# A linear-attention and expert-attention kernel: another source for its filler matmuls, and another cut of its first batch

## The chip, the cores and the metric

The kernel runs on one core of one Trainium2 chip. Its engines run side by side, each through its own list of instructions in order: TensorE (PE in the profile; PEld are its weight loads), VectorE (DVE), ScalarE (ACT), GpSimd (POOL) and SyncE (SP), which here issues all transfers (DMA). The metric is device microseconds of one execution; less is better.

## The reference

Two stages. First a linear attention with a complex decay for each channel, for 4 batches, 8 heads, 768 steps and 48 channels a head:

```python
mag = np.sqrt(a_re * a_re + a_im * a_im)
scale = np.minimum(mag, 0.999) / (mag + 1e-06)
a_re_n, a_im_n = (a_re * scale, a_im * scale)
for t in range(S):
    new_re = ar * S_re - ai * S_im          # ar, ai: step t of a_re_n, a_im_n
    new_im = ar * S_im + ai * S_re
    S_re, S_im = (new_re + k_t v_t^T, new_im)
    y[:, :, t] = q_t S_re
```

Its output, 768 steps by 384 columns for each batch, is the x of the second stage: four experts, each a causal softmax attention (`wq`, `wk`, `wv`, `wo`, 64 columns), added up for each step with the weights of the two experts that a gate (`w_gate`) ranks highest.

## The kernel before

**The first stage, in chunks.** The decay is written as magnitude and angle: their running sums over a chunk turn q and k into decayed, rotated q and k, and what is left are matmuls over chunks of 128 steps. The 384 columns lie as three groups j of 128 partitions. Elementwise work on `ab` (the decays) and `qk` goes through the helpers `quotients`, `arcs`, `magnitudes`, `angles`, `sines`, `products`, on VectorE, ScalarE and GpSimd. `regroup` (transfers `fm<-qk`) puts the columns of two heads together (four pairs g; pair 0 lies in group j=0 alone, pair 1 in j=0 and 1, pair 2 in j=1 and 2, pair 3 in j=2). For each pair and each k (256 steps, two chunks) `head` transposes k (`pk`, to `kts`) and makes the chunk's scores (`psc`, masked to `pts` with `keep`), `state` makes the carried state (`pu`, `sum`, `tst`), and `tail` the output (`yu`, to `x`; pair 3 goes by `yt` and transfers `x<-yt`).

**The second stage**, `moe(b)`: `proj` makes q and k of two experts at a time (`pp`, to `qka`), 512 and then 256 steps wide, nine matmuls each; `vproj` (`pv`) the values and the gate's logits; `maxpass` the row maxima (`pm`, `mx`), `mrow` (`pmr`) turns them; then `score` (`psS`, to `pe`), `av` (`po`), `total` (`dn`), `norm`, `wo` (`pw`).

**The order.** No helper issues an instruction at once. `Work` collects them as a numbered list, and `run` issues them in the order of the written list `ORDER`, a permutation of all of them. Each engine's instructions follow each other in that order, and SyncE's transfers too. `ROOMS` says which of its buffers each tile gets. `WARM` says ahead of which numbers how many filler matmuls (`warm`) are put: 128 by 128 weights, 512 columns, into a PSUM bank that nobody reads. There are 244 of them; 172 stand ahead of number 171, the first matmul of the first `head`. What they read is set by

```python
    nc.warm = keep, mask[:, :512]
```

where `keep` and `mask` are made from `iota` by VectorE: `keep` (number 2) is at place 178 of `ORDER`, among the elementwise work, `mask` at 7 and 104.

In the first batch the elementwise work is cut: `quotients` and `arcs` for all three groups, for k=0 and then for k=1 and 2 together, then the other helpers and the heads k by k. The batches 1 to 3 go group by group, all 768 steps at once. Loads are SyncE's first instructions: `ab` and `qk` of the first batch in two parts (k=0; k=1 and 2), the weights `wst`, and `vt`.

Of the kernel before, what the change touches and what calls it, by code (L numbers as in the profile page):

```python
# [390 lines left out]
def attention_moe(ctx: ExitStack, tc: tile.TileContext, ak, vk, w, out):  # L391
# [489 lines left out]
    for g in range(NP):  # L881
        load_v(0, g)
    load_w()
    for c in PARTS:
        for f in (quotients, arcs):
            for j in range(3):
                f(0, j, *c)
# [76 lines left out]
```

## Time and profile before

| | us |
|---|---|
| median of the runs shown (3) | 502.98 |
| lowest and highest of them | 499.4, 504.44 |
| the profiled execution | 498.99 |
| its span, first to last instruction | 497.3 |

| engine | busy us | share of the span | instructions |
|---|---|---|---|
| TensorE, matmuls | 437.3 | 88% | 3720 |
| VectorE | 338.4 | 68% | 788 |
| ScalarE | 332.2 | 67% | 762 |
| GpSimd | 239.2 | 48% | 225 |

Between the profiled execution's time and its span lie 1.7 us. The profile's page has the sum for each engine, the span in 40 slices, and the chain of work that ended last; the views of the trace (timeline, waits, windows, groups by form) show single instructions. Times in them count from the span's start.

### The profile page before, as it was taken

How to read it: one execution, taken by the hardware profiler on the slowest of the kernel's cores; microseconds unless marked ns; L12 is line 12 of the kernel's file. 1: busy time of each engine (PE TensorE's matmuls, PEld its weight loads, DVE VectorE, ACT ScalarE, POOL GpSimd, SP SyncE). 2: the span in 40 equal slices, each digit the busy share in tenths (PEclk: the TensorE clock that was granted, in tenths of full speed). 3: DMA queues.
4: the chain of work that ended last, by engine and by line, in shares of the span. 5: the costliest groups of instructions: out<-in, count | busy, mean ns of one | idle time of the engine just before them, and what ended most of it. 6: DMA issues, size and time to landing. Idle time of an engine off the chain costs nothing.

```text
span 497.3 us, 10026 instructions
## 1 busy us (share of the span) xinstructions
PE 437.3 (88%) x3720; PEld 334.0 (67%) x3720; DVE 338.4 (68%) x788; ACT 332.2 (67%) x762; POOL 239.2 (48%) x225
## 2 busy tenths in 40 slices
PE   0009999899898899999898999999999999999995
PEld 0004446777658667787797877878988887887565
DVE  4793007858876999985388989778887752566711
ACT  5992006859966888886685899867868556234453
POOL 3643004425842457769732379847434416302780
PEclk9999999999999989999899999999999999999999
DMA  8901003575187827218345492366405302001002
GB/s 286 347 1 42 1 0 85 154 205 141 21 227 172 194 87 171 87 28 212 65 120 152 96 242 96 92 158 180 109 12 125 97 7 59 18 32 65 18 1 95
DMA packets 22943, 53.46 MB, mean 107 GB/s; under 512 B 3344, under 2 KB 9584, under 8 KB 22768
## 3 DMA queue, kind: packets, MB, share of 16 engines
q1 hardware_dynamic: 22896, 52.83, 38.9%
q8 instruction: 29, 0.48, 0.4%
q14 instruction: 18, 0.15, 0.1%
HBM read 26.74 MB, written 4.72 MB: 63 GB/s over the span
## 4 chain that ended last, share of the span: by engine, by line
PE 60%; ACT 11%; DVE 11%; DMA 7%; POOL 4%; issue 3%; SPq 2%; POOLq 0%; DVEq 0%; ACTq 0%
PE psS L387 9%; PE warm L380 9%; PE pp L387 7%; PE po L387 7%; PE yu L387 6%; PE psc L387 6%; ACT qk L387 5%; PE pw L387 4%; PE pu L387 3%; DVE qk L387 3%; PE pv L387 3%; ACT ab L387 3%; PE pm L387 2%; DMA ab<-in_ak_dram 2%; SPq L387 2%
## 5 line engine op out<-in xcount | busy, mean ns | idle before, releaser
L380 PE MATMUL warm<-mask,keep 128*128 128x512 bf16 x244 | 58.3, 392 | 37.6 <-DVE carry L387 37.5
L387 POOL TENSOR_TENSOR pe<-pe 128x512 f32<-128x512 f32 (+1 forms) x64 | 80.5, 1259 | 20.6 <-PE po L387 17.7
L380 PEld LDWEIGHTS <-keep 128*128 128x128 bf16 x244 | 24.0, 101 | 66.3 <-DVE keep L387 37.5
L387 DVE TENSOR_TENSOR pts<-psc,keep 128x512 f32<-128x512 f32 x48 | 32.7, 682 | 44.7 <-PE psc L387 42.2
L387 ACT ACTIVATE ab<-ab 128x768 f32<-128x768 f32 (+2 forms) x90 | 56.5, 644 | 8.4 <-DVE ab L387 4.7
L387 ACT ACTIVATE qk<-qk 128x768 f32<-128x768 f32 (+3 forms) x126 | 59.7, 500 | 2.6 <-DVE qk L387 2.1
L387 POOL TENSOR_TENSOR qk<-qk,ab 128x256 f32<-128x256 f32 (+1 forms) x24 | 29.4, 1226 | 60.8 <-ACT ab L387 52.1
L387 ACT ACTIVATE pe<-psS 128x512 f32<-128x512 f32 (+2 forms) x96 | 47.3, 542 | 16.9 <-PE psS L387 14.1
L387 PE MATMUL psc<-fm 96*128 96x128 f32 x384 | 54.2, 286 | 2.0 <-ACT kts L387 1.0
L387 POOL TENSOR_TENSOR qk<-qk 128x768 f32<-128x768 f32 (+1 forms) x27 | 36.4, 1354 | 38.2 <-ACT qk L387 37.6
L387 POOL TENSOR_SCALAR_AFFINE_SELECT pe<-pe 128x256 f32<-128x256 f32 x48 | 26.3, 561 | 57.6 <-ACT pe L387 55.9
L387 DVE CUSTOM_DVE_ANT_0 pm<-pm,mask 128x384 f32<-128x384 f32 (+4 forms) x96 | 46.9, 512 | 10.0 <-PE pm L387 9.8
L387 PEld LDWEIGHTS psc<-fm 96*128 96x128 f32 x384 | 47.3, 194 | 7.8 <-ACT kts L387 2.3
L387 ACT ACTIVATE kts<-pk 128x384 f32<-128x384 f32 (+1 forms) x48 | 20.3, 431 | 44.9 <-PE pk L387 44.7
L387 PE MATMUL pp<-x,whi 128*128 128x512 f32 (+1 forms) x192 | 45.2, 353 | 5.4 <-DMA x<-yt 4.0
L387 ACT ACTIVATE tst<-sum,fm 96x48 f32<-96x48 f32 x128 | 38.9, 326 | 16.3 <-DVE sum L387 16.2
L387 PE MATMUL psS<-qka 64*128 64x256 f32 (+3 forms) x480 | 46.9, 303 | 0.1
L387 PE MATMUL po<-pe,v 128*64 128x256 f32 (+3 forms) x320 | 45.4, 397 | 0.0
L387 PEld LDWEIGHTS psS<-qka 64*128 64x128 f32 x480 | 37.2, 185 | 7.0 <-issue 3.0
L387 DVE TENSOR_TENSOR qk<-qk,ab 128x768 f32<-128x768 f32 (+1 forms) x48 | 39.8, 844 | 3.0 <-POOL qk L387 1.7
L387 PE MATMUL yu<-pts,vt 128*64 128x128 f32 x384 | 37.7, 281 | 2.2 <-DVE pts L387 1.6
L387 PEld LDWEIGHTS pp<-x,whi 128*128 128x128 f32 x192 | 31.7, 194 | 11.4 <-DMA x<-yt 4.1
(105 smaller groups left out, 977.2 us busy)
## 6 DMA issues: line engine op xcount, KB each, us to landing
fm<-qk SPq DMA_DIRECT2D x18, 578.2 KB
ab<-in_ak_dram SPq DMA_DIRECT2D x9, 768.0 KB
qk<-in_ak_dram SPq DMA_DIRECT2D x9, 768.0 KB
vt<-in_vk_dram SPq DMA_DIRECT2D x16, 384.0 KB
fm<-qk SPq DMA_DIRECT2D x24, 192.8 KB
out_dram<-ob SPq DMA_DIRECT2D x24, 192.0 KB
fm<-qk SPq DMA_DIRECT2D x6, 385.5 KB
x<-yt SPq DMA_DIRECT2D x72, 32.0 KB
```

Of the source, the lines that this page charges most:

```text
L380: chain("tensor", nc.tensor.matmul(x, *map(real, self.warm), start=True, stop=True))
L387: chain(engine, getattr(getattr(nc, engine), method)(*map(real, a), **{x: real(y) for x, y in k.items()}))
```

## The change

1. A tile `src` (128 by 512, bf16) is cleared by GpSimd as number 0 of the list and at place 0 of `ORDER`; the filler's weights and columns are both read from it. `keep` and `mask` are made as before, for their own use.
2. The first batch's elementwise work is cut another way: group j=0 for k=0 goes through all helpers, its regroup, and the head of pair 0; then groups 1 and 2 for k=0 with the pairs 1, 2, 3; then all groups for k=1 and 2 together, and the heads for both.
3. The first batch's projections go 256, 256 and 256 steps wide in place of 512 and 256, with `vproj` and `maxpass` of the chunks behind each.
4. `ORDER`, `ROOMS` and `WARM` are new throughout. Filler: 242 matmuls, 151 of them ahead of the first head's first instruction (number 72, place 170), 35 ahead of the first `vproj` (number 1080, place 326). SyncE issues 211 transfers, from 219; the loads of `qk` for k=1 and 2 of group 1 (number 32) go from place 81 to place 301.

```diff
@@ ORDER: the first lines
-    15, 21, 17, 8, 14, 9, 19, 3, 23, 29, 20, 27, 22, 28, 37, 0, 42, 33, 10, 44, 34, 43, 54, 26, 46, 45, 55, 47, 84, 57, 76, 24, 75, 108, 109,
...
@@ ORDER, ROOMS: all other lines
...
 WARM = {
-    171: ("psu_4", 172), 185: ("psu_4", 1), 193: ("psu_4", 11), 225: ("psu_4", 3), 252: ("psu_4", 1), 266: ("psu_4", 2), 452: ("psu_4", 1), 392:
-    ("psu_4", 1), 616: ("psu_4", 4), 1130: ("psu_4", 4), 644: ("psu_3", 3), 639: ("psu_3", 2), 838: ("psu_0", 23), 906: ("psu_1", 6), 1330:
-    ("psu_1", 2), 1377: ("psa_1", 1), 4413: ("psa_0", 3), 4419: ("psa_0", 4),
+    72: ("psu_4", 151), 1080: ("psu_4", 35), 390: ("psa_1", 8), 410: ("psu_4", 2), 420: ("psa_0", 3), 540: ("psu_4", 2), 1147: ("psa_2", 11),
+    1287: ("psa_2", 5), 1180: ("psa_2", 3), 840: ("psu_2", 4), 843: ("psu_1", 4), 1298: ("psu_4", 1), 1345: ("psa_1", 5), 1406: ("psu_0", 2),
+    4381: ("psa_1", 3), 4387: ("psa_1", 3),
 }
...
-PARTS = [(0, 1), (1, 3)]
+
+PARTS = [((0,), 0, 1, (0,)), ((1, 2), 0, 1, (1, 2, 3)), ((0, 1, 2), 1, 3, (0, 1, 2, 3))]
...
+    src = new([128, 512], BF, "src")
+    nc.gpsimd.memset(src, 0.0)
+    nc.warm = src[:, :C], src
     iota = new([128, 128], F32, "iota", "ob")
...
-    nc.warm = keep, mask[:, :512]
...
-        for n0, n1 in ((0, 512), (512, S)):
+        spans = ((0, C2), (C2, 512), (512, S)) if b == 0 else ((0, 512), (512, S))
+        for n0, n1 in spans:
             for off, hi, lo in ((WK, 3, 0), (WQ, 1, 2)):
                 proj(0, off, hi, lo, n0, n1)
...
-        for n0, n1 in ((0, 512), (512, S)):
+        for n0, n1 in spans:
             for off, hi, lo in ((WK, 3, 0), (WQ, 1, 2)):
                 proj(1, off, hi, lo, n0, n1)
...
+    for js, k0, k1, gs in PARTS:
+        for f in (quotients, magnitudes, arcs, angles, sines, products):
+            for j in js:
+                f(0, j, k0, k1)
+        for g in range(NP):
+            regroup(0, g, k0, k1, js)
+        for k in range(k0, k1):
+            for g in gs:
+                head(0, g, k)
+                state(0, g, k)
+                tail(0, g, k)
     load_w()
-    for c in PARTS:
-        for f in (quotients, arcs):
-            for j in range(3):
-                f(0, j, *c)
-    for k in range(NK):
-        for f in (magnitudes, angles, sines, products):
-            for j in range(3):
-                f(0, j, k, k + 1)
-        for g in range(NP):
-            regroup(0, g, k, k + 1)
-        for g in range(NP):
-            head(0, g, k)
-            state(0, g, k)
-            tail(0, g, k)
```

## Rows read from the trace of the kernel before

**Rows 1.** The page: span and parts 1 and 2 (40 slices, busy tenths).

```profile
span 497.3 us, 10026 instructions
...
PE 437.3 (88%) x3720; PEld 334.0 (67%) x3720; DVE 338.4 (68%) x788; ACT 332.2 (67%) x762; POOL 239.2 (48%) x225
...
PE   0009999899898899999898999999999999999995
DVE  4793007858876999985388989778887752566711
```

**Rows 2.** Windows: length, busy PE, PEld, DVE, ACT, POOL, PEclk, DMA, GB/s; last row `warm` alone.

```profile
0.00:37.50 37.50, 0.01 (x1) 0.02 (x2) 28.03 (x62) 32.08 (x85) 17.39 (x26) 1.00 0.57 210
37.50:76.40 38.90, 38.90 (x172) 17.35 (x173) 4.13 (x10) 3.35 (x12) 4.13 (x7) 1.00 0.05 14
76.40:183.30 106.90, 97.32 (x776) 73.39 (x774) 86.78 (x185) 83.51 (x192) 49.25 (x40) 0.98 0.55 143
183.30:497.30 314.00, 301.07 (x2773) 243.28 (x2773) 219.47 (x535) 213.29 (x475) 168.38 (x153) 0.99 0.36 95
...
76.40:183.30 106.90, 17.13 (x65) 0.98 0.55 143
```

**Rows 3.** Timeline 36.5 to 39.5: start us, us, engine line op out<-in xcount [idle before <-releaser].

```profile
...
36.68 0.74 DVE L387 TENSOR_SCALAR keep<-iota 128x128 bf16<-128x128 f32 x1
...
37.48 0.13 PEld L380 LDWEIGHTS <-keep 128*128 128x128 bf16 x2 [37.48 <-DVE keep L387]
...
38.06 2.01 SPq L387 DMA_DIRECT2D fm<-qk  x3
```

**Rows 4.** Timeline of TensorE's matmuls, 36 to 77 us.

```profile
37.49 39.08 PE L380 MATMUL warm<-mask,keep 128*128 128x512 bf16 x172 [37.49 <-DVE carry L387]
76.40 1.06 PE L387 MATMUL psc<-fm 96*128 96x128 f32 x8
```

**Rows 5.** Waits that end in 76 to 184: total us, times, longest us.

```profile
DVE pts L387 <- PE psc L387: 37.9, 5, 35.6
```

**Rows 6.** Timeline of the program's start, GpSimd and VectorE.

```profile
0.90 0.15 POOL L387 IOTA tie<- 128x16 f32 x1 [0.40 <-POOLq L953]
...
1.36 0.33 DVE L387 MEMSET mask<- 128x320 uint32 x1
```

**Rows 7.** Timeline of the filler's weight loads (one of nine slow ones, then 18).

```profile
38.31 0.15 PEld L380 LDWEIGHTS <-keep 128*128 128x128 bf16 x1 [0.28 <-issue]
...
41.22 3.77 PEld L380 LDWEIGHTS <-keep 128*128 128x128 bf16 x18 [0.20 <-issue]
```

**Rows 8.** Chain that ended last: start us, us, what; L385 is a table load.

```profile
...
104.72 5.33 DMA ab<-in_ak_dram
...
122.61 1.28 ACT L385
...
135.35 4.92 DMA qk<-in_ak_dram
...
151.60 3.67 DMA x<-yt
...
240.22 2.61 DMA x<-yt
```

**Rows 9.** A group by form, 0 to 45 us (busy us, mean ns | idle before), then ScalarE's timeline.

```profile
L387 ACT ACTIVATE qk<-qk 128x256 f32<-128x256 f32 x40 | 13.6, 401 | 0.1
...
35.52 0.49 ACT L387 ACTIVATE ab<-ab,col 128x256 f32<-128x256 f32 x1
```

**Rows 10.** Timeline of projections' matmuls, 512 and 256 columns, by threes.

```profile
138.07 0.86 PE L387 MATMUL pp<-x,wlo 128*128 128x512 f32 x3
...
159.46 0.51 PE L387 MATMUL pp<-x,whi 128*128 128x256 f32 x3
```

**Rows 11.** Window 176 to 182 us (columns as rows 2), then `psc` in it.

```profile
176.00:182.00 6.00, 5.90 (x34) 3.81 (x35) 5.50 (x20) 5.98 (x12) 2.55 (x2) 0.72 0.01 2
...
177.49 1.95 PE L387 MATMUL psc<-fm 96*128 96x128 f32 x8
```

412 rows, old and new, of tables (ORDER, ROOMS) are left out of this document.

## The prediction, written before the changed kernel ran

> **What bounds the kernel now.** I read the page first: TensorE is busy for 88% of 497.3 us, more than any other engine, yet in the slices of the first part its row shows nine tenths and more while VectorE's falls to nothing for three [rows 1]. So I cut the span at the places where that begins and ends. From 37.50 to 76.40 us TensorE is busy for all of 38.90 us with 172 matmuls, and VectorE, ScalarE and GpSimd are busy for 3 to 4 us each; DMA moves almost nothing [rows 2]. The 172 matmuls are the filler (`warm`), and the first real matmul, `psc`, starts at 76.40 [rows 4]. Filler does no work of the result. It keeps TensorE busy ahead of the first tile; but its weights are `keep`, which VectorE writes at 36.68, behind nearly the whole front of the first batch; the load of the weights waits for just that, and starts at 37.48 [rows 3]. Two microseconds later the first tile is on its way: its two transfers `fm<-qk` are issued at 38.06 and about 0.7 later [rows 3]. So the first tile waits behind 39 us of filler, and all else waits for the first tile: `pts` on VectorE waits 35.6 us for `psc` [rows 5]. That stall is the largest single thing in the trace. Ahead of it (0 to 37.5) ScalarE is the busiest (32.1 of 37.5). Behind it, up to the first scores at 183.30, VectorE and ScalarE are busy for 86.8 and 83.5 of 106.9 us and TensorE also runs 17.1 us of filler; after 183.30 TensorE is busy for 301 of 314 us and is the bound [rows 2].
>
> **The change, part by part.** *The filler's source.* The filler now reads `src`, which GpSimd clears as its first instruction. The trace has no such memset; GpSimd's first instruction of the kernel starts at 0.90, and took 0.15 us for 16 columns; a VectorE memset of 320 words took 0.33 [rows 6]. `src` has 256 words or 512 columns, as one counts: between 0.15 and, by 512/320 of 0.33, 0.53 us, I take 0.4, and filler starts at about 1.4 us. Its weight loads came 0.43 us apart for nine matmuls, then 18 in 3.77 us, 0.21 apart [rows 7]; 172 took 38.9 us in all [rows 2], so a fast one takes (38.9 - 9 x 0.43) / 163 = 0.215, and 151 need 38.9 - 21 x 0.215 = 34.4 us, and end at about 36. What becomes of the first tile without the stall? Its transfers are issued at 38.06 and 38.8; the nearest transfers with a shown landing, `x<-yt`, took 2.6 and 3.7 us [rows 8]. It would be there at 41.4 to 42.5 instead of 76.4: 33.9 to 35.0 us won, which agrees with VectorE's wait. I take **34.5**. The cover that hides the filler from then on is the first batch's elementwise front: filler that ends at 36 is over before any tile is there.
>
> *The first tile ahead of the others.* `PARTS` runs group j=0 of the first 256 steps through all its steps first, then its head. Walking both orders up to the second sine of that group, the last thing ScalarE does for it, 81 ScalarE instructions become 62; with each form's own time in the trace (13.6 us of busy time for 40 of the commonest [rows 9]) 27.9 us of ScalarE become 25.8. VectorE's share falls from 26.3 to 21.2 and GpSimd's by 1, so ScalarE stays the one that counts. That sine ended at 36.0 [rows 9] and would end at 33.9, the first tile be there at 39.3 to 40.4: **2.1** won. If ScalarE were no bound there, the bounds are 0 and 5 us (VectorE's saving).
>
> *From the first tile to the first scores.* Counted along the two orders, VectorE has 87 us of work between those points before and after; ScalarE has 72 and 71, and 9 and 7 table loads of 1.28 us [rows 8]. Fewer and wider instructions (steps 1 and 2 of the first batch are now done together) take another 3 us of VectorE out of the whole. So this stage, 106.9 us now, gets **3** shorter by the table loads; no more, since VectorE's sum is the same. It can be more: the chain through it holds transfers that somebody waits for, `ab` of the next batch (5.33 us) and `qk` (4.92) [rows 8]; in the new order the first of these is issued after 40 us of VectorE's work instead of 51, and its first user comes at 46 instead of 58. If both go off the chain, 10 more are won. It can be less: 35 filler matmuls (7.5 us at 0.215) now stand ahead of the first `vproj`, covered only by the wait for `x<-yt`; if that cover is gone, they cost all of it. In total the stage holds 77 filler matmuls after and 65 before, much the same.
>
> *Projections and maxima by thirds.* In the first batch 36 matmuls of 512 columns become 72 of 256. Three of 512 last 0.86 us, three of 256 0.51 [rows 10]: 24 x 0.51 less 12 x 0.86 is 1.9 us as the upper bound; the lower one is 0, since each of these times ends with a tail over which the next three already run. I take **+0.5** us, nearer to nothing, as TensorE is not the bound there; four more evictions of 0.4 us on ScalarE lie beside other work. What it buys, work for TensorE from the first third on, is not on the bound of that stage, so I count nothing for it.
>
> *The new order behind the first scores.* From there VectorE has 219 us left before and 220 after, ScalarE 194 and 196 and TensorE as many matmuls (2121 and 2122). No row prices a permutation; I take 0, with 3 us to either side, 1% of 314.
>
> *A point against the change.* Filler ends at 36 and the first tile comes at 39.3 or later, so TensorE idles for 3 to 4 us, where now filler runs right into the tile. The trace shows what a fallen clock costs: in 176 to 182 us the granted clock is 0.72, that is, part of it at 1.2 GHz instead of 2.4, and the eight `psc` matmuls at 177.49 take 1.95 us where the first eight at 76.40 took 1.06 [rows 4, 11]. At such a price a fall here costs 1 to 2 us of a stage that TensorE does not bound: 0. The Trainium skill (TensorE: Matmul & The Clock Gate, Part 1: The HAM clock gate) says that the low clock is the array's default, that activity lifts it and idle time lets it fall; by that rule the tile would start at the low clock and the sum be 1 to 2 us longer.
>
> The sum, against the profiled execution's own 499.0 us (span 497.3 and 1.7 around it): 499.0 - 34.5 - 2.1 - 3 + 0.5 = 459.9. The profiled execution lies at the low end of the runs shown (499.4, 503.0, 504.4), 4 us under their median; a median of the changed kernel should lie about 1 us over such a sum too: **461 us**.
>
> **The rivals.** *The order gives some back.* The load of group j=1's second part of `qk` goes from place 81 of the order, ahead of all regroups, to place 301; there it stands behind the first regroups and four `x<-yt`, that wait for TensorE's first tiles, and GpSimd's two multiplications, the products and the regroup of that group wait for it. Such a load takes about 5 us [rows 8]; with the 7.5 us of filler uncovered beside it, up to 12 are lost: 470 to 475, and with the stage behind also off by 1% to 480. For it: one wait of this kind stopped all engines in the old order. Against: VectorE has 16 us of other work between the first head and that point.
>
> *More is won:* both transfers off the chain, -10, and 1% behind the scores: 446 to 452. For it: TensorE gets projections of the first third early. Against: VectorE's sum.
>
> *The change does not do what it says:* filler still starts at about 37.5, since something else that it waits for comes late. Then only the 21 filler matmuls that are left out are won, 4.5 us, and 3 of the stage: 499 - 7.5 = 491.5, and 493 for a median. From a start at 5 us on (39.3 less 34.4) each microsecond of delay costs one. Against it: the weight load waited for `keep` alone [rows 3], and `src` has nothing ahead of it.
>
> *Slower than before:* the clock stays at 1.2 GHz between the first tile and the scores, because TensorE is idle more often there once its filler is moved. Without filler it is busy for 97.3 - 17.1 = 80 us there [rows 2]. Matmuls twice as long would add up to 80 us; with 27 us of gaps in the stage (106.9 - 80) taken first, 53. Slower than before needs the 39 that are won to be lost, which is from about 66 us at the low clock on. Against it: 0.98 is granted in that stage now, gaps and all [rows 2], and it will hold about as much filler.
>
> **How the numbers follow.** The sum as it stands, 452 to 469: 0.73. Some given back, 469 to 480: 0.13. More won, below 452: 0.09. Filler still late: 0.02. Slower: 0.02. Something near no change, by several of these together: 0.01. A measurement of this kernel can tell about 1% from no change, 5 us. All of the first four lie more than that under 503, so faster has 0.97, same 0.01, slower 0.02. The range reaches from 449, most of the case that wins more, to 475, half of the one that gives back.
>
> **What would show it.** Right: filler starts before 2 us and ends at 35 to 37; the first `pk` or `psc` at 38.5 to 41; no wait over 10 us of VectorE and ScalarE on it; first scores at 138 to 146; from these to the end 311 to 317 us. Wrong: a filler whose weights wait for anything but `src`; idle stretches of VectorE behind the first tile that end on a `qk` load or on the 35 filler matmuls; a clock under 0.9 between 40 and 140 us; or a tail from the first scores that is off by more than 5 us, which this sum puts at nothing.

## The result, and the profile of the changed kernel

The first four executions of the changed kernel took 474.05, 467.47, 484.18 and 482.91 us: a median of 478.48, against 501.19 for the kernel before beside them. The ratio is 0.9387, with a 95% interval of 0.9236 to 0.9538. Six more executions in a later comparison had a median of 471.20 (463.90 to 473.25) against 506.93; ratio 0.9263, 0.9138 to 0.9387. The ratios leave out executions that are over 1.5% above the fastest of the same kernel; since these are here the ones that lost most clock, which turns out to be the point of the case, medians and spreads below are over all executions. So the change is faster, by 4.5% (the first medians) to 7.4% (the later ratio). The forecast was 461, range 449 to 475: the second median lies inside, the first 3.5 us above, and they lie 17.5 and 10.2 us over the forecast.

Below, **lost clock** is (1 - granted clock) x span of an execution: a stretch wholly at 1.2 instead of 2.4 GHz counts with half its length.

The page of after: the span, part 1, and of part 2 (40 slices of 11.8 us) the rows of TensorE, VectorE and the granted clock.

```profile
span 472.3 us, 9992 instructions
...
PE 453.0 (96%) x3754; PEld 350.8 (74%) x3754; DVE 335.7 (71%) x768; ACT 328.7 (70%) x731; POOL 236.0 (50%) x214
...
PE   8998999999998999998999999999999999999896
...
DVE  3977548778789899774999895878965543666622
...
PEclk9997599979969999999999999999959999999999
```

The empty stretch of [rows 1] is gone. What is new is the clock's row: dips in the fourth and fifth slice, the ninth, the twelfth and the thirtieth. The windows of after tell where (columns as in [rows 2]; the last two rows are the whole stage from first tile to first scores, and filler alone in it).

```profile
0.00:38.10 38.10, 35.11 (x151) 15.29 (x151) 26.84 (x53) 31.37 (x72) 15.90 (x25) 1.00 0.58 206
38.10:60.00 21.90, 21.54 (x132) 18.42 (x133) 15.13 (x25) 8.18 (x24) 5.17 (x5) 0.55 0.21 51
60.00:100.00 40.00, 38.90 (x311) 29.54 (x309) 29.21 (x64) 34.11 (x81) 19.92 (x15) 0.97 0.65 171
100.00:120.00 20.00, 20.00 (x154) 17.00 (x153) 16.08 (x32) 12.84 (x25) 9.54 (x7) 0.87 0.29 80
120.00:155.10 35.10, 32.11 (x229) 25.05 (x227) 28.80 (x66) 24.20 (x52) 15.23 (x11) 0.85 0.64 154
155.10:472.30 317.20, 305.32 (x2784) 245.54 (x2784) 219.67 (x533) 218.06 (x481) 170.22 (x154) 0.98 0.36 97
...
38.10:155.10 117.00, 112.56 (x821) 90.00 (x821) 89.21 (x184) 79.32 (x180) 49.87 (x37) 0.84 0.50 128
...
38.10:155.10 117.00, 19.88 (x78) 0.84 0.50 128
```

Filler now lies beside the elementwise front (first row). The first tile is at TensorE at 38.18 instead of 76.40, 38.2 us earlier, but the span is only 25.0 shorter: the stage up to the first scores (at 155.06) takes 116.9 instead of 106.9, and the tail 317.3 instead of 314.0. VectorE and ScalarE are busy in the stage for about as long as in [rows 2] (89.2 and 79.3 us against 86.8 and 83.5); TensorE's busy time has grown from 97.3 to 112.6 us, at a clock of 0.84 instead of 0.98. TensorE's timeline of after shows how:

```profile
1.38 35.11 PE L380 MATMUL warm<-src 128*128 128x512 bf16 x151 [1.38 <-POOL src L387]
38.18 0.27 PE L387 MATMUL pk<-ident,fm 96*128 96x96 f32 x1 [1.69 <-DMA fm<-qk]
...
39.04 1.08 PE L387 MATMUL psc<-fm 96*128 96x128 f32 x8
...
43.16 1.97 PE L387 MATMUL psc<-fm 96*128 96x128 f32 x8
...
57.80 0.64 PE L387 MATMUL yu<-fm,tst 96*48 96x128 f32 x4
58.37 1.89 PE L380 MATMUL warm<-src 128*128 128x512 bf16 x4
```

Filler ends at 36.49, TensorE waits 1.69 us for the tile, and the first eight `psc` still run as in [rows 4] (1.08 us). Then the clock is at 1.2 GHz for 20.5 us from 40.3 on: the next eight take 1.97. It comes back behind the 35 filler matmuls that start at 58.37.

The later profile of the very same kernel is the comparison, as its fall there lasted 3.4 us instead of 20.5:

```profile
38.10:60.00 21.90, 20.95 (x160) 15.30 (x162) 17.88 (x30) 13.16 (x34) 8.99 (x8) 0.92 0.32 80
60.00:141.70 81.70, 76.64 (x654) 61.91 (x659) 66.95 (x156) 65.47 (x147) 39.36 (x28) 1.00 0.63 162
141.70:461.30 319.60, 306.54 (x2782) 247.07 (x2784) 219.99 (x533) 218.66 (x481) 172.65 (x155) 0.98 0.36 96
```

Its TensorE timeline:

```profile
38.15 0.27 PE L387 MATMUL pk<-ident,fm 96*128 96x96 f32 x1 [1.30 <-DMA fm<-qk]
...
43.07 1.74 PE L387 MATMUL psc<-fm 96*128 96x128 f32 x8
...
46.91 1.16 PE L387 MATMUL psc<-fm 96*128 96x128 f32 x8
...
53.12 7.07 PE L380 MATMUL warm<-src 128*128 128x512 bf16 x32 [0.16 <-issue]
```

The same four heads are through at 53.1 instead of 58.4, the first scores come at 141.69 instead of 155.06, and the span is 461.3. One program, two executions, 11 us apart: the stage differs by 13.3, the tail by 2.3 the other way.

### The profile page after: what moved, and what is told of

The parts are those of the page before. It is cut to its first block, busy times and chain, and to the rows that moved or that the text cites. A ratio compares the mean times of both kernels' runs of the same rounds, so it can differ in the third digit from the quotient of the medians.

```text
span 472.3 us, 9992 instructions
## 1 busy us (share of the span) xinstructions
PE 453.0 (96%) x3754; PEld 350.8 (74%) x3754; DVE 335.7 (71%) x768; ACT 328.7 (70%) x731; POOL 236.0 (50%) x214
## 4 chain that ended last, share of the span: by engine, by line
PE 58%; ACT 15%; DMA 9%; DVE 5%; POOL 5%; SPq 4%; issue 3%; POOLq 0%; ACTq 0%; DVEq 0%
PE pp L387 8%; PE psc L387 8%; PE yu L387 7%; PE psS L387 7%; PE pw L387 5%; ACT qk L387 5%; PE pv L387 5%; PE pu L387 5%; DMA fm<-qk 4%; ACT ab L387 4%; PE po L387 4%; SPq L387 4%; PE pm L387 3%; PE pk L387 3%; DMA ab<-in_ak_dram 3%
## 5 line engine op out<-in xcount | busy, mean ns | idle before, releaser
L387 POOL TENSOR_TENSOR pe<-pe 128x512 f32<-128x512 f32 (+1 forms) x64 | 83.9, 1311 | 16.7 <-PE po L387 13.3
L387 ACT ACTIVATE pe<-psS 128x512 f32<-128x512 f32 (+2 forms) x96 | 47.9, 540 | 22.2 <-PE psS L387 19.3
L387 PE MATMUL psc<-fm 96*128 96x128 f32 x384 | 60.5, 312 | 1.1 <-DVE sum L387 0.4
L380 PE MATMUL warm<-src 128*128 128x512 bf16 x242 | 58.5, 397 | 1.4 <-POOL src L387 1.4
L387 ACT ACTIVATE qk<-qk 128x768 f32<-128x768 f32 (+5 forms) x105 | 57.4, 563 | 1.1 <-DVE qk L387 0.7
L387 PEld LDWEIGHTS psc<-fm 96*128 96x128 f32 x384 | 54.4, 220 | 3.9 <-issue 0.9
L387 DVE CUSTOM_DVE_ANT_0 pm<-pm,mask 128x384 f32<-128x384 f32 (+4 forms) x96 | 47.2, 511 | 12.3 <-PE pm L387 11.8
L387 POOL TENSOR_SCALAR_AFFINE_SELECT pe<-pe 128x256 f32<-128x256 f32 x48 | 22.7, 485 | 63.6 <-ACT pe L387 31.3
L387 POOL TENSOR_TENSOR qk<-qk 128x768 f32<-128x768 f32 (+2 forms) x24 | 36.7, 1542 | 32.8 <-ACT qk L387 30.8
L387 PE MATMUL pp<-x,whi 128*128 128x256 f32 (+1 forms) x216 | 46.6, 328 | 3.6 <-ACT ob L387 2.0
L387 POOL TENSOR_TENSOR qk<-qk,ab 128x768 f32<-128x768 f32 (+2 forms) x19 | 28.7, 1510 | 39.4 <-ACT ab L387 20.9
L380 PEld LDWEIGHTS <-src 128*128 128x128 bf16 x242 | 23.6, 102 | 31.0 <-issue 6.1
L387 DVE TENSOR_TENSOR pts<-psc,keep 128x512 f32<-128x512 f32 x48 | 32.8, 683 | 17.5 <-PE psc L387 15.3
L387 DVE TENSOR_TENSOR qk<-qk,ab 128x768 f32<-128x768 f32 (+2 forms) x41 | 38.5, 960 | 9.3 <-ACT ab L387 8.0
L387 POOL TENSOR_SCALAR ab<-ab 128x768 f32<-128x768 f32 (+2 forms) x24 | 22.3, 931 | 37.0 <-DVE ab L387 19.0
```

The lines of the kernel that those rows point to most:

```text
L380: chain("tensor", nc.tensor.matmul(x, *map(real, self.warm), start=True, stop=True))
L387: chain(engine, getattr(getattr(nc, engine), method)(*map(real, a), **{x: real(y) for x, y in k.items()}))
```

## Experiments

Two theories. **A:** the predicted mechanism holds, and what is missing is TensorE's clock, which is lost more often once the stall is gone. **Rivals:** the order or the thirds cost time by themselves; the new filler's data does it; filler in the stage costs TensorE time. All kernels in one table; front is filler ahead of the first tile, behind is the rest; times are medians (lowest to highest) in us; lost is the mean lost clock over the executions; ratios are to the kernel before on the same chip, where one could be formed. (An expectation below counts 94 behind the front of after; the lists of `WARM` give 91, and 72 for before.)

| kernel | front + behind | time | lost | ratio, 95% interval |
|---|---|---|---|---|
| after | 151 + 91 | 478.5 (467.5 to 484.2) | 26.2 | 0.939, 0.924 to 0.954 |
| after again | 151 + 91 | 471.2 (463.9 to 473.3) | 16.2 | 0.926, 0.914 to 0.939 |
| source alone | 172 + 72 | 472.7 (467.4 to 478.1) | 10.9 | 0.936, 0.927 to 0.946 |
| old source | 151 + 91 | 490.5 (478.4 to 500.0) | 14.7 | none |
| 160 at the front | 160 + 91 | 472.6 (461.2 to 478.3) | 16.2 | none |
| 35 spread | 151 + 91 | 478.3 (473.5 to 488.9) | 22.7 | 0.958, 0.946 to 0.969 |
| 74 more | 160 + 165 | 470.3 (469.5 to 471.2) | 2.7 | 0.943, 0.936 to 0.950 |
| ones | 151 + 91 | 478.2 (468.2 to 487.3) | 25.8 | 0.945, 0.929 to 0.961 |
| front only | 151 + 0 | 484.4 (474.5 to 487.5) | 45.8 | none |
| no filler | 0 + 0 | 492.3 (489.6 to 496.2) | 40.3 (see below) | 0.987, 0.977 to 0.997 |
| late groups | 160 + 120 | 467.1 (464.6 to 471.5) | 7.9 | 0.933, 0.918 to 0.948 |
| singles | 160 + 112 | 466.9 (466.2 to 469.2) | 6.9 | 0.933, 0.925 to 0.941 |
| late groups again | 160 + 120 | 464.0 (462.2 to 469.6) | 5.0 | 0.920, 0.913 to 0.926 |

What joins them is the spread inside each kernel. Spans of single executions, with lost clock behind the @:

```
before             495.6@3.5  497.5@3.5  499.8@6.0  503.1@7.0  504.3@5.0  505.3@9.1  503.5@12.1
after              465.4@13.5 472.3@24.1 480.0@32.6 482.2@34.7
after again        461.3@8.8  467.6@15.9 468.1@15.9 470.7@16.9 469.5@19.2 470.8@20.7
160 at the front   459.4@5.1  467.9@12.6 473.8@22.7 476.6@24.3
old source         476.5@1.9  487.7@12.2 488.9@17.1 498.3@27.4
```

Straight lines through these rows have slopes of 0.82, 0.79, 0.81, 0.83 and 0.83 us of span for a microsecond lost, and meet zero loss at 495.9, 454.2, 454.8, 455.9 and 475.6. So each kernel has a full-clock span, and pays about 0.8 us for every one lost. (Single slopes scatter: the kernel before has 1.22, 0.65 and 0.65 in its three other sets of executions, the other kernels lie between 0.4 and 1.6. One slope for all 88 executions with a clock on record, each kernel and set about its own mean, is 0.77, with a 95% interval of 0.70 to 0.85.) The Trainium skill (TensorE: Matmul & The Clock Gate, section HAM oscillation — how this bites in real kernels) prices a throttled stretch at half its length, which is a slope of 1 in these terms; the measured 0.8 is a little below it, presumably as some of the slower matmuls lie beside other work, which no run isolates.

### The source alone, and the source undone

The kernel before with `src` as the filler's operands, all the rest as it was:

```diff
+    src = new([128, 512], BF, "src")
+    nc.gpsimd.memset(src, 0.0)
+    nc.warm = src[:, :C], src
     iota = new(
...
-    nc.warm = keep, mask[:, :512]
```

> The kernel before with the new filler source alone: src is cleared first, its order and its 172 filler matmuls stay. Clock theory (the new kernel misses the sum because TensorE's clock falls behind the first tile, where its filler between the heads was taken out): here the filler runs into the first tile and the fillers between the heads stay, so the clock stays up as before (0.99 granted) and the time is 499 to 503 less 34.5, 464 to 468, that is faster than the whole change. Order theory (the clock is a side effect; waits of the new order eat the gain): the same 464 to 468, but the clock plays no part in the difference. If the stall was not what I took it for, the time stays above 485.

```profile
42.80 1.71 PE L366 MATMUL psc<-fm 96*128 96x128 f32 x8 [2.01 <-DMA fm<-qk]
```

Its median was 472.7, where 464 to 468 were expected: the filler did not run into the first tile, as the expectation had it, but left a gap of 2.01 us. The first tile came at 42.80, and its profile's stage took 116.1 us with 20.5 us at the low clock. So the early filler alone brings all that can be told from the whole change in these medians. The rest of the change isn't nothing: at like loss its executions lie above the kernel after (466.1 at 8.9 lost against 461.3 at 8.8; 476.4 at 15.2 against 467.6 at 15.9), by 5 to 9 us, though on two chips and by two single executions. But the kernel after loses more clock, 26.2 and 16.2 us against 10.9, and pays that gain back.

The opposite: the kernel after with the old operands.

```diff
-    nc.warm = src[:, :C], src
...
+    nc.warm = keep, mask[:, :512]
     col = new([128, 4], F32, "col")
```

> The changed kernel with the filler reading keep and mask again, its order and counts as changed (src is left out): the source undone. keep then is written at about 28 us, the filler of 151 ends at 28 + 34.4 = 62, and the first tile waits from 38 to 62: 24 us more than the changed kernel at an equal clock. Clock theory: the elementwise work gets ahead during the stall, but the heads run as slowly; 495 to 500. If the source does not matter in the new order: the same as the changed kernel.

TensorE's timeline, and its stage as a window:

```profile
24.74 35.56 PE L380 MATMUL warm<-mask,keep 128*128 128x512 bf16 x151 [24.74 <-DVE keep L387]
60.14 0.49 PE L387 MATMUL pk<-ident,fm 96*128 96x96 f32 x4
...
60.10:163.00 102.90, 96.79 (x822) 75.65 (x820) 83.52 (x181) 78.01 (x177) 45.14 (x33) 1.00 0.54 140
```

`keep` is written earlier in the new order, so filler starts at 24.74 rather than 37.48, and the first tile waits for it until 60.14, 22.0 us later than after. The full-clock spans differ by as much (475.6 against 454.2). With the stall the stage runs at 1.00 in this profile and takes 102.9 us: that is the length of the new order and the thirds when the clock holds and work has piled up ahead of it, 4 us less than in [rows 2]. The median, 490.5, lies under the 495 to 500 expected. This run also limits theory A: with a stall in place three of its four executions lost 12.2 to 27.4 us of clock, and the mean of 14.7 is about that of the kernel after in its later executions, 16.2. In the old order, taking the stall away raised the mean from 6.6 to 10.9. So the new order with its own filler can lose clock with a stall ahead of it too, and how much of the clock the stall had saved isn't settled.

### Where the clock is lost: the gap before the first tile, and a thin stage

Nine filler matmuls more at the front:

```diff
-    72: ("psu_4", 151), 1080: ("psu_4", 35), ...
+    72: ("psu_4", 160), 1080: ("psu_4", 35), ...
```

> The changed kernel with 160 filler matmuls ahead of the first tile in place of 151, so that no gap is left (filler ends at 38.4, the tile is there at 38.2 to 38.7). If the 1.7 us gap lets the clock fall: it stays up from 40 to 60 us and the time falls by 8 us or more. If the small matmuls of the heads, with no filler between them, let it fall: the clock falls at about 40 us as before and the time is the same within 3 us. Order theory: the same within 3 us.

Its TensorE timeline and windows:

```profile
37.98 0.27 PE L400 MATMUL pk<-ident,fm 96*128 96x96 f32 x1 [0.26 <-DMA fm<-qk]
...
38.00:60.00 22.00, 20.27 (x164) 14.11 (x164) 18.51 (x31) 13.97 (x39) 8.94 (x8) 1.00 0.36 89
60.00:118.00 58.00, 55.00 (x462) 44.54 (x462) 45.29 (x96) 44.44 (x100) 29.02 (x21) 1.00 0.59 153
118.00:154.80 36.80, 33.74 (x193) 27.05 (x193) 27.87 (x60) 22.68 (x44) 13.54 (x9) 0.63 0.49 119
```

The gap shrinks from 1.69 to 0.26 us and the fall at 40 is gone. Over all profiles of kernels with early filler at the front this holds: gaps of 1.30, 1.69, 1.98, 2.01, 2.25 and 2.69 us were each followed by a fall at 39 to 43 us, gaps of 0.00, 0.26, 0.26, 0.45 and 0.76 by none. But this profile then lost the clock for 23.9 us from 120.8 on, in heads of the second batch, and its span was no shorter. The median, 472.6, can't be told from that of the kernel after: the expected gain was had in one place and lost in another.

The 35 filler matmuls in front of the first `vproj`, dealt out to the heads of the first tiles instead:

```diff
-    1080: ("psu_4", 35)
+    1080: ("psu_4", 8), 168: ("psu_4", 9), 195: ("psu_4", 9), 222: ("psu_4", 9)
```

> The changed kernel with the 35 filler matmuls ahead of the first vproj spread: 9 ahead of the heads of pairs 1, 2 and 3 each and 8 ahead of vproj, the count kept. Clock theory: the granted clock from 40 to 60 us stays near 1 (0.56 in the changed kernel), the heads take half the time, and the time falls by 6 to 10 us, if the elementwise work then is not the bound. Order theory: the heads wait for the elementwise work anyway, the time stays within 3 us or rises by up to 6 (27 fillers of 0.215 us in the path).

No gain: 478.3, 22.7 lost. Its gap before the tile was 2.25 us and the clock fell at 39.4, but for 6.8 us only; then, with 8 filler matmuls instead of 35 in the wait for `x<-yt`, TensorE waited 3.45 and 3.41 us there and the clock fell again at 66.7. The 35 had been covering a wait, so moving them uncovered it.

### What the filler multiplies, and what it buys

```diff
-    nc.gpsimd.memset(src, 0.0)
+    nc.gpsimd.memset(src, 1.0)
```

> The kernel after with the filler's source filled with 1.0 instead of 0.0, all else the same. Theory A (the fall comes from the gaps and the short matmuls of the stage, not from what the filler multiplies): as the kernel after, first fall at about 40 us, lost clock 13 to 35 us, a median of 470 to 485. Rival D (zeros keep the clock up less well than the old source's mask did): lost clock as before the change, under 10 us, a median of 458 to 465.

478.2 and 25.8 lost, like the first executions of the kernel after: these runs show no difference by the data.

With only the 151 at the front left, `WARM = {72: ("psu_4", 151)}`:

> The kernel after with the 151 filler matmuls ahead of the first tile only; the 94 behind it are left out. Theory A: the stage from first tile to first scores runs at the low clock for 60 us or more, lost clock 35 to 60 us, span 454 + 0.8 x 35 to 60, less up to 5 for filler that stood in the way: a median of 480 to 500. Rival B (filler in the stage only takes TensorE's time): 10 to 15 us faster than the kernel after, 460 to 468.

```profile
38.50:174.10 135.60, 117.41 (x743) 102.44 (x745) 91.74 (x184) 81.38 (x181) 50.09 (x37) 0.63 0.44 111
```

The 19.9 us of filler that after's windows show in the stage are out, and yet TensorE is busy for longer, as the clock is 0.63. 484.4 us: by the medians, filler in the stage is worth 6 to 13 us more than it costs. Beside the kernel with ones, which ran in the same rounds, the 6 lie inside the scatter of four executions each.

Without any, `WARM = {}`:

> The kernel after without any filler. Theory A: as the kernel with filler only at the front, and a low clock from the first tile on: 480 to 505, and still not slower than the kernel before, whose stall it does not have. Rival B (filler buys nothing once the tile is early): 455 to 468. The difference to the kernel with filler at the front alone is what the 151 early filler matmuls buy by themselves; theory A expects 0 to 5 us, since the clock falls again 2 us behind the first tile anyway.

492.3 us, 8 slower than with the front's filler, where up to 5 were expected; still 1.3% faster than before, whose filler, stall and order all differ, so that this doesn't price before's filler by itself. Its windows, and TensorE's timeline (the helper's line is 384 here):

```profile
38.50:60.00 21.50, 21.42 (x128) 19.23 (x128) 13.52 (x23) 6.75 (x20) 5.12 (x5) 1.00 0.22 52
60.00:86.00 26.00, 15.95 (x120) 14.70 (x118) 15.73 (x29) 17.75 (x45) 12.16 (x10) 1.00 0.63 167
86.00:118.00 32.00, 31.22 (x187) 27.11 (x186) 19.95 (x48) 21.76 (x45) 10.55 (x9) 0.52 0.27 80
...
39.51 1.97 PE L384 MATMUL psc<-fm 96*128 96x128 f32 x8
...
44.78 1.97 PE L384 MATMUL psc<-fm 96*128 96x128 f32 x8
```

Here the clock column misleads: it says 1.00 from 38.5 to 60, but eight `psc` take 1.97 us, which is the low clock's time. The trace has no record of the clock before 73.2 us, and the column then reads 1.00. So this kernel's lost clock is counted too low, in this profile by about 17 us (an estimate: half of the time from 38.5 to 73, where three `pv` quicken from 0.85 to 0.52 us). The Trainium skill (TensorE: Matmul & The Clock Gate, Part 1: The HAM clock gate) warns that records of the clock can be unreliable; this run agrees, 1.00 beside 1.97 us.

### How much filler: three doses

74 more in 21 groups of 3 to 6, on top of the 160 (an extract):

```diff
+    173: ("psu_0", 3), 200: ("psu_0", 3), 227: ("psu_0", 3), 395: ("psu_4", 3), 425: ("psu_4", 3),
...
+    707: ("psa_0", 3), 734: ("psu_0", 4), 759: ("psu_0", 4), 762: ("psu_4", 4), 1209: ("psu_3", 6), 2950: ("psu_2", 4),
```

> The kernel after with 160 instead of 151 filler matmuls ahead of the first tile, and 74 more of them in 21 small groups of 3 to 6 ahead of heads and maxima, at those places of 42 to 152 us and of 344 to 350 us where the clock fell in the runs so far. Theory A (the miss is the clock: at full clock the kernel needs about 456 us of span, and each microsecond of clock that is lost costs about 0.8): mean lost clock falls from the 16 us of the kernel with 160 filler to 8 or less, spans of 458 to 466, a median of 463. Rival B (TensorE's time in the stage is itself on the path, so filler costs what it lasts): 74 x 0.215 = 15.9 us more, a median of 480 to 490. Rival C (the clock falls whatever TensorE does): lost clock as before, 12 to 25 us, a median of 470 to 480.

```profile
38.40:153.90 115.50, 109.10 (x889) 81.87 (x887) 91.74 (x183) 79.73 (x180) 49.91 (x37) 1.00 0.51 130
...
38.40:153.90 115.50, 36.38 (x146) 1.00 0.51 130
```

Both sides were half right. The clock holds (2.7 lost, executions within 1.7 us of one another), but the stage is as long as after's: 36.4 us of it are filler, and the span without loss rose from 456 to 467, 0.15 us for each added matmul of 0.215. Filler in this stage isn't free.

29 in 12 groups, nearly all in the second batch's heads, and one each at the 21 places:

```diff
+    558: ("psu_0", 2), 1128: ("psa_1", 3), 707: ("psa_0", 3), 734: ("psu_0", 2), 759: ("psu_0", 2), 762: ("psu_4", 3),
+    783: ("psu_2", 2), 788: ("psu_1", 2), 815: ("psu_4", 2), 1209: ("psu_3", 4), 2950: ("psu_2", 2), 3005: ("psu_1", 2),
```

> The kernel after with 160 filler matmuls ahead of the first tile and 29 more in 12 small groups, nearly all of them (25) behind 118 us, ahead of the heads and maxima of the second batch, where the kernel with 160 filler lost its clock first. The 74 of the earlier run cost 11 us at full clock (467 against 456), 0.15 us each; so 29 cost 4.4. Theory A (filler costs time on TensorE and pays by keeping the clock, and these places are the ones that lose it): lost clock under 6 us, spans of 460 to 466, a median of 465. Rival (the clock is lost at other places as well, which differ from one execution to the next): lost clock 10 to 20 us, spans of 464 to 477, a median of 472.

> The kernel after with 160 filler matmuls ahead of the first tile and a single one more at each of the 21 places that had 3 to 6 of them in the earlier run with 74 more: cost at full clock 21 x 0.15 = 3.2 us. Theory A with the places as what counts: lost clock under 6 us, spans of 459 to 465, a median of 464. Rival (one matmul at a place is too little to keep the clock there): lost clock 10 to 25 us as with 160 filler alone, a median of 470 to 476.

467.1 with 7.9 lost and 466.9 with 6.9: both keep most of the clock, if not to under 6 as expected, at under half the price (taken back to no loss at 0.8 a microsecond, both are at 460, where 160 at the front alone is at 456 and the 74 are at 467). Theory A's medians, 465 and 464, were 2 to 3 us too low. Last, the first of these in the same rounds as the kernel after:

> The kernel with 160 filler matmuls at the front and 29 more in 12 late groups once more, now on the same chip and in the same rounds as the kernel after. Theory A: lost clock of 4 to 12 us, a median of 464 to 469, and 8 to 15 us less than the kernel after beside it. Rival (the differences so far are between chips and days, not between kernels): within 4 us of the kernel after.

> The kernel after unchanged, beside the kernel with 29 more filler matmuls. Theory A: spans of 454 + 0.8 x lost clock with 13 to 35 us lost, that is 465 to 483, a median of 474 to 482. Rival: a median within 4 us of the kernel beside it, with little clock lost.

464.0 against 471.2, where 474 to 482 were expected of the latter. The means of six are 464.5 and 470.2, a difference of 5.7 us with a 95% interval of 1.8 to 9.7 from their scatter: less than the 8 expected at least, as the kernel after lost less clock than in its first executions, but a gain. Stage and tail of its profile:

```profile
38.00:146.00 108.00, 100.58 (x837) 78.00 (x846) 87.33 (x184) 79.04 (x180) 49.57 (x37) 1.00 0.55 139
146.00:462.60 316.60, 304.20 (x2785) 244.70 (x2788) 219.53 (x533) 218.35 (x481) 170.72 (x154) 0.99 0.36 97
```

This version beats both kernels: 0.920 of the kernel before, 0.913 to 0.926. How much of the gain is due to the 29 and how much to the nine more at the front isn't separated, as 160 at the front alone did not run beside them.

## Why the prediction was right, and where it was not

**The filler's source: right.** Start at 1.38 (forecast 1.4), 151 matmuls in 35.11 us (34.4), end at 36.49 (about 36). The rival that it stays late is out.

**The first tile: right, a little early.** 76.40 less 36.6 is 39.8; it came at 38.18. The source alone gave 42.80, where 41.4 to 42.5 was worked out, and the rest of the change 4.6 us instead of 2.1: near the bound of 5 us that VectorE's saving set.

**The stage: right at the clock that the sum took for granted, wrong at the clock that was granted.** Forecast 106.9 - 3 + 0.5 = 104.4 us. The later profile, with 3.4 us of the stage at the low clock, has 103.5, and the old source's 102.9 with none. The first profile has 116.9 with 37.5 at the low clock.

**The thirds: as priced, by rows.** In after's chain nine projections of 256 columns take 1.06 us and nine of 512 take 2.08; 72 of the former are 8.5 us and 36 of the latter 8.3, inside the forecast's 0 to 1.9. The thirds and the first tile ahead weren't run without the new order, for which the kernel has only one list of places.

**The tail: 314 plus or minus 3 forecast, 317.3 and 319.6 measured,** both at 0.98, with 10.2 us at the low clock from 344.1 and 13.7 from 331.1 on; the tail of before had 3.4. The second is 5.6 over, past the 5 us that the prediction named as a sign of being wrong. Where such a stretch is short, in the last kernel run, it is 316.6 with 7.8.

**The step that failed** is the one headed *A point against the change*. It saw the gap between filler and first tile, and the fall that followed, priced it at 1 to 2 us, and counted 0 "of a stage that TensorE does not bound". The mechanism was there (with a gap of 1.69 us instead of 3 to 4); its size was off, for two reasons. The sign of being wrong that the prediction named, a clock under 0.9 between 40 and 140 us, came in the first profile (0.81) and not in the later one (0.98).

First, the fall was taken as a matter of one group of matmuls. In the row it drew on, [rows 11], the low clock lasted 3.4 us; in after it lasted 20.5 from the first tile on, and came back at two more places of the stage.

Second, "TensorE does not bound the stage" was read from sums of busy time, 80 us without filler against VectorE's 87 [rows 2]. The chain of waits says otherwise as soon as the clock is low. By line, over the stage, first after, then the later profile of the same kernel:

```profile
by line: PE psc L387 14.1%; PE yu L387 11.2%; PE warm L380 7.6%; PE pu L387 6.9%; issue 6.8%; DMA fm<-qk 6.7%; DVE qk L387 5.9%; PE pk L387 4.6%; ACT ab L387 4.4%; DMA qk<-in_ak_dram 4.2%; PE pp L387 3.6%; PE pv L387 2.9%; ACT qk L387 2.7%;
```

```profile
by line: DVE qk L387 10.1%; PE pp L387 10.0%; ACT ab L387 6.7%; ACT qk L387 6.7%; DMA fm<-qk 6.7%; PE yu L387 6.2%; DMA x<-yt 5.6%; PE psc L387 5.4%; issue 5.3%; PE pv L387 4.8%; SPq L387 4.7%; ACT L385 4.2%; ACT tst L387 4.0%; PE pk L387 2
```

In the first TensorE's heads lead (`psc`, `yu`, `pu`, `pk`); summed over all its 168 pieces, TensorE holds 61.6 of 116.9 us. In the second it holds 31.6 of 103.6, and VectorE and ScalarE together 47.9; in the kernel before it held 19.1 of 106.9, and they 50.5. So even with the clock up TensorE is on the path for a third of the new stage. An engine that is nearly as busy as the leading one becomes the bound when it slows by a part.

So the sum is right for the clock of the kernel before and short by the clock term. Its span, 458.2 (460 less 1.7 around it), was made from a profile with 3.5 us lost; the line of the kernel after gives 454.2 + 0.79 x 3.5 = 457.0 there. The first four executions lost 26.2 on average, where before lost 6.6 beside the first experiments: (26.2 - 6.6) x 0.79 = 15.5 us, of the 17.5 by which their median missed. In the later six it was (16.2 - 9.8) x 0.81 = 5.2, of 10.2; on that chip before, too, took 506.9 rather than 503, and after's time lay 2.2 us over its span on average instead of 1.7. That the second median is in the range and the first is not hangs on the lost clock, for which the sum has no term: to that extent the hit is luck. Both lie outside the sum's own band, 452 to 469 with 0.73, and in the next, 469 to 480 with 0.13.

**The rivals.** *Slower than before* had the mechanism and put its point of decision at 66 us at the low clock. That is mis-worked: the 39 that are won and the 27 of gaps are 66 us added to TensorE's time, and at half the clock it takes 132 us to add them. In after's profile 37.5 us of the stage were at the low clock, with no filler behind the front 99.5, and even then the kernel was faster than before. *The order gives some back:* its number fits, 470 to 480, but its causes hardly do. The late `qk` load is issued at 62.00 and held GpSimd up for 2.0 us; the 35 filler matmuls lie in the wait for `x<-yt`, since without them TensorE waits 5.02 and 3.24 us there, though in the first profile, where they run in part at the low clock, they stand on the chain with 8.8 us. *More is won:* no execution was under 452, and by the line above even the full-clock span would be 454.

**Still open:** why the clock falls in one execution and holds in the next. The gap before the first tile goes with the fall at 39 to 43 in every profile of a kernel with early filler. The later falls look alike; in after, for one, the clock fell at 344.1 behind this wait:

```profile
342.64 0.47 PE L387 MATMUL pk<-ident,fm 96*128 96x96 f32 x3 [1.16 <-DMA fm<-qk]
```

Over all profiles, of 36 falls from 66 us on (the last 10 us left out) 30 came in a wait of TensorE of 0.9 us or more, or at most 3 us behind one. But of 81 such waits at the full clock only 31 were followed by a fall, so a wait alone doesn't decide it. The longest low stretches lie in heads with little else on TensorE, and a few filler matmuls there went with less lost clock.

## What to carry to other kernels

When a stall is taken away, ask what becomes of the clock: here one execution showed 25 us of the 39 that were forecast, and another 35. That work piled up behind the stall had kept TensorE at 2.4 GHz is a guess that the old source's profile fits (1.00 behind 22 us of stall) and its other executions don't (12.2 to 27.4 us lost). Price a slower clock on every engine that is busy for nearly as long as the leading one, and compare kernels at equal lost clock before judging an order. Filler is a trade: each matmul cost 0.15 us in this stage and each lost microsecond 0.8, so few are enough: 38 more, nine at the front and most others where the clock falls, made the kernel 5.7 us faster, and 83 more, with a median of 470, showed no further gain.

## What was not expected of the hardware

- The clock stayed low while TensorE was hardly idle. In after it fell behind a wait of 1.69 us and then stayed at 1.2 GHz to 60.8, although TensorE was busy for 21.54 of 21.90 us from 38.10 on. The Trainium skill (TensorE: Matmul & The Clock Gate, Part 1: The HAM clock gate) has the low clock follow on idle time, and activity lift it: the trace agrees with the fall behind the gap, and shows that a TensorE that the profile calls busy can stay low. Without filler, 21 us of heads (busy 21.42 of 21.50) never lifted it, by the 1.97 us of `psc`.
- One program differed by 17 us of span between executions (465.4 to 482.2), with 13.5 to 34.7 us of clock lost; with 74 more at the thin places they lay within 1.8 us of one another.
- Filler on ones lost 25.8 us of clock and filler on zeros 26.2 and, in its later executions, 16.2: no difference that these runs can tell.
